# Attention, feed-forward and mixture of experts in one kernel: decay products moved from GpSimd to VectorE and ScalarE, routing of the last group moved and rearranged

## The chip, the cores and the metric

The kernel runs on one core of a Trainium2 chip. The metric is the time of one execution in microseconds of the device. Its engines are TensorE (matmuls, PE in the profile, its weight loads PEld), VectorE (DVE), ScalarE (ACT), GpSimd (POOL) and SyncE (SP), which issues most of the transfers. Each engine takes its instructions in order and waits where one needs what another has not finished.

## The reference

Three layers follow each other on B x S = 2 x 768 tokens of width 512 (8 heads of 64).

```python
# 1. linear attention with decay lam per head, in blocks
intra = (q k^T * Dmask) v                     # Dmask: lam ** (i - j), 0 above the diagonal
inter = (q * lam ** (i + 1)) state
state = lam ** block * state + (k * lam ** (block - 1 - j))^T v
# 2. feed-forward 512 -> 2048 -> 512
h = x @ w_in ; g = maximum(0.01 * h, h) ; x = g @ w_out        # weights are float64
# 3. eight experts, one per token
logits = x @ w_gate + modality_bias[modality_id]
e = argmax(logits) ; gate_w = softmax(logits)[e]
out = gate_w * (relu(x @ w1[e]) @ w2[e])
```

## The kernel before, in words

**Work and order.** The 1536 tokens are 12 chunks of 128, chunk 2j and 2j+1 make group j of 256 tokens. The feed-forward layer has 16 slices of 128 columns, so there are 96 units u = 16 j + f. The main loop goes over them; a unit is ff1 (12 matmuls, the fp32 product as three products of rounded parts, L406) into one of two banks, then L409 on ScalarE (0.01 h), L414 on VectorE (the maximum), L421 on ScalarE (the high part), L422 on VectorE (the low part), and, two units later, ff2 (6 matmuls, L435). Since the two banks alternate, ff1 of a unit waits for L414 of the unit two before it. The units of groups 0 and 1 alternate in the loop, the rest follow group by group. Nothing reorders the instructions: each engine's queue is as the code is written, and the engines run apart as far as the tiles allow.

**Conversion.** The feed-forward weights come as float64 bits and are turned into fp32 high and low parts inside the loop, one tile per unit from the fourth unit to the 26th (the "conversion ring" below): three bit steps on VectorE (L1494, L1499 twice), the rounding on ScalarE (L1504) and, one unit later, the difference on VectorE (L1506). The first tiles are converted ahead of the loop or several to a unit.

**Attention.** Its pieces are hooks: `at(j, f, fn, ...)` puts a call behind unit 16 j + f, called a slot here. `at_first` computes the scores of a chunk (L304), multiplies qT with the decay powers lq (`at_prep_q`, L281) and the scores with the decay matrix (`at_mask`, L317). `at_prep_k` multiplies k with its decay (L294 on GpSimd, L290 on ScalarE for chunks 2 and 3). `at_out` makes the chunk's output (L333, L343), which is staged (L345) or split into the parts xh and xl (L357, L358). `at_state` forms k^T v (L372) and multiplies the state with its decay (L378, GpSimd), `at_state_add` adds the two (L392). k and v have one buffer each, so that a chunk's k is loaded only after the state of the chunk before it has read its own. The two chunks of a group are dealt with in the group before.

**Routing.** Behind a group's last unit `evac_x2` copies its accumulators to the tile x2s (L461, L463) and writes them to memory. Since x2s has one buffer, the copy waits for what read the group before, its gate's write (L571) among it. The accumulators of odd groups lie in banks 3 and 4, those of even groups in 5 and 6, and the scores of later chunks take over such banks. `route_dot` makes the 16 dot products of a group with the gate's rows (two tiles, eight experts, L516), `route_v1` the one-hot of the largest, `route_rk` the ranks on TensorE from it (L546), `route_v2` the position from the ranks (L579 to L586), and `route_gate` the gate's factor (L561 to L571). RSLOT gives for each group the slot of its first dots, the step of experts per slot, the slot of v1, and the slot of the rest. In the last group of the main loop but one (group 4, whose dots fall into group 5's units), half of the dots are a product on GpSimd (L521) and a sum on ScalarE.

**First expert weights.** During group 5 the weights of the most frequent expert are loaded and split (`split_w`: L876 on ScalarE, L877 on VectorE or GpSimd), its tokens are indexed (`early_idx`), gathered (`first_gather`) and transposed (`TX`).

Of the kernel before, what the change touches and what calls it, by code (L numbers as in the profile page):

```python
# [21 lines left out]
C = 128  # L22
# [4 lines left out]
NSTAT = 10  # L27
NPLAIN = 12
NAR = 32
PREP_ACT = (2, 3)  # L30
KV = {1: 'wo15', 2: 'wi15', 3: 'wo14'}
QK = {2: 'wi14', 3: 'wo13'}
NPOS = {2: 0, 3: 1, 4: 2}
# [7 lines left out]
def tile_attention_ffn_moe(  # L41
# [235 lines left out]
    def at_prep_q(n):  # L277
        b, c = ORD[n]
        t = chunks[n]
        if c > 0:  # L280
            nc.gpsimd.tensor_mul(out=t["qT"], in0=t["qT"], in1=lq)  # L281

    def at_prep_k(n):
        b, c = ORD[n]
        t = chunks[n]
        if c + 1 >= NCH:
            return
        if n in PREP_ACT:
            for h in range(H):
                nc.scalar.activation(  # L290
                    out=t["k"][:, h, :], in_=t["k"][:, h, :], func=AF.Copy, scale=dec[:, h, C - 1:C]
                )
        else:
            nc.gpsimd.tensor_tensor(  # L294
                out=t["k"], in0=t["k"], in1=dec[:, :, C - 1:C].to_broadcast([128, H, D]), op=ALU.mult
            )

    def at_scores(n, b0, b1):
        t = chunks[n]
# [60 lines left out]
    def at_state(n, bk):  # L360
        b, c = ORD[n]
        if c + 1 >= NCH:
            return
        t = chunks[n]
        o = bank(bk, "as")
        kd = t["k"].rearrange("p h d -> p (h d)")
        vv = t["v"].rearrange("p h d -> p (h d)")
        for g in range(4):
            for half in range(2):
                p0 = half * 64  # L370
                cs = slice(g * 128 + p0, g * 128 + p0 + 64)
                nc.tensor.matmul(o[p0:p0 + 64, cs], lhsT=kd[:, cs], rhs=vv[:, cs], start=True, stop=True)  # L372
        t["so"] = o
        if c > 0:
            for half in range(2):
                p0 = half * 64
                sl = state[b][p0:p0 + 64, :, p0:p0 + 64]
                nc.gpsimd.tensor_tensor(  # L378
                    out=sl, in0=sl, in1=lq[p0:p0 + 64, :, C - 1:C].to_broadcast([64, 4, 64]), op=ALU.mult
                )  # L380

    def at_state_add(n):
# [126 lines left out]
    def route_dot(j, jobs):  # L509
        if j not in lgs:  # L510
            lgs[j] = sm.tile([128, 2, E], F32, tag="lgs", name="lgs")
        for e, tk, buf in jobs:
            xv = x2s[j][tk][:, 0:512]
            acc = lgs[j][:, tk, e:e + 1]
            if buf is None:
                nc.vector.scalar_tensor_tensor(  # L516
                    out=junk, in0=xv, scalar=1.0, in1=wgr[e], op0=ALU.mult, op1=ALU.mult, accum_out=acc
                )
            else:
                pr = qkv_p.tile([128, 512], F32, tag=buf, name="pr", bufs=1 if buf in ("v", "k") else 2)  # L520
                nc.gpsimd.tensor_mul(out=pr, in0=xv, in1=wgr[e])  # L521
                nc.scalar.activation(out=pr, in_=pr, func=AF.Copy, accum_out=acc)
# [769 lines left out]

    V, P = nc.vector, nc.gpsimd
    nc.sync.dma_start(out=lam_sb, in_=lam.rearrange("(h o) -> h o", o=1))
    load_chunk(0, ("qT", "kT"))
    load_win(0)
    make_dec()
    store_dec()
    load_wout(0)
# [76 lines left out]
        xt_split(n, chunks[n]["kT"])  # L1376

    at(0, 7, at_first, 4, 2, 7)
    at(0, 7, at_prep_k, 4)
    at(0, 8, at_out, 4, 7, True)  # L1380
    at(0, 9, at_state, 4, 2)
    at(0, 9, load_chunk, 5, ("v", "k"))
    at(0, 10, at_state_add, 4)
    at(0, 11, at_first, 5, 2, 7)
    at(0, 11, at_prep_k, 5)
    at(0, 12, at_out, 5, 7, True)
    at(0, 13, at_state, 5, 2)
    at(0, 14, at_state_add, 5)
# [3 lines left out]
    at(0, 15, load_chunk, 7, ("qT", "kT"))  # L1392


    at(2, 9, lambda: evac_x2(1))
    at(3, 2, lambda: evac_x2(2))

    SLOT = {
        2: (None, 2, 5, 7, 10, 10, 12, 13, 15),
# [1 line left out]
    for j in range(2, last):  # L1401
# [4 lines left out]
            at(j, s_ld, load_chunk, n, ("qT", "kT", "v", "k"))  # L1406
            at(j, s_ld, load_chunk, n + 1, ("qT", "kT"))
        at(j, s_a, at_first, n, *((2, 7) if j == 2 else sb))
        at(j, s_a, at_prep_k, n)
        at(j, s_o, at_out, n, 7)  # L1410
        at(j, s_s, at_state, n, 2)
        at(j, s_s, load_chunk, n + 1, ("v", "k"))
        at(j, s_s, at_prep_k, n + 1)
        at(j, s_d, at_state_add, n)
        at(j, s_a2, at_first, n + 1, *sb)
        at(j, s_o2, at_out, n + 1, 7)
# [1 line left out]
        at(j, s_d2, at_state_add, n + 1)  # L1418


    RSLOT = {0: (32, 1, 39, 40), 1: (41, 1, 48, 49), 2: (51, 1, 58, 59), 3: (66, 1, 73, 74), 4: (82, 2, 87, 88)}
    for r, (f0, step, fv, fr) in RSLOT.items():
        for i in range(0, E, step):
            jobs = [(e, tk, None) for e in range(i, i + step) for tk in range(2)]
            if r == last - 1:
                jobs = [(e, tk, ("v", "k")[e % 2] if tk else None) for e, tk, _ in jobs]
            at(0, f0 + i // step, route_dot, r, jobs)
        at(0, fv, route_v1, r)
        at(0, fr, route_rk, r, 7)
# [268 lines left out]
```

## Time and profile before

| | before |
|---|---|
| time, median of 3 runs | 526.44 us (526.16 to 526.71) |
| profiled execution | 525.76 us, of which the span is 523.7 |
| mean granted clock of TensorE | 0.979 |
| TensorE (PE) busy | 493.7 us, 94% |
| VectorE busy | 319.6 us, 61% |
| ScalarE busy | 174.1 us, 33% |
| GpSimd busy | 105.7 us, 20% |

The profile is of one execution, and its times count from the start of the span. Busy time is the time in which an engine worked; TensorE's can hold overlapped matmuls. The profile's rows give a number in brackets where an engine sat idle before an instruction, and what released it. A row of several instructions ("x4") has the time from the first one's start to the last one's end.

### The profile page before, as it was taken

The numbers are of one execution on the slowest core, as the hardware profiler recorded it, in microseconds if no ns is written. First come the engines' busy times: TensorE is split into PE (matmuls) and PEld (weight loads), VectorE is DVE, ScalarE is ACT, GpSimd is POOL, SyncE is SP. The second block draws the span as 40 slices with busy tenths as digits, with TensorE's granted clock in tenths as the row PEclk, the third lists the DMA queues.
The fourth block names the chain that finished last, engine by engine and source line by source line (L and its number), as shares of the span: only waits on it lengthen the run. The fifth ranks groups of instructions, "written<-read, shape, count | busy, mean of one in ns | idle before, by whom it ended". The sixth has DMA issues, their size and how long they took to land. (4 is left out here: it accounts for less than half of the span.)

```text
span 523.7 us, 9395 instructions
## 1 busy us (share of the span) xinstructions
PE 493.7 (94%) x3485; PEld 420.6 (80%) x3485; DVE 319.6 (61%) x767; ACT 174.1 (33%) x409; POOL 105.7 (20%) x142
## 2 busy tenths in 40 slices
PE   5769999999999999999999998999999999999994
PEld 3657978788988888888988897887788987879693
DVE  4798998998576787774577458864551252513130
ACT  2155434344322223223322335453222254322221
POOL 1220021212021211021022045260231212323111
PEclk8879999999999999999999998999999999999998
DMA  7999301703601102110400035211169509173101
GB/s 252 364 406 401 125 1 48 251 1 104 224 1 42 41 1 86 58 40 2 140 23 22 0 123 197 44 43 41 39 234 398 182 21 347 63 249 143 41 2 42
DMA packets 30667, 63.41 MB, mean 121 GB/s; under 512 B 6871, under 2 KB 8799, under 8 KB 30608
## 3 DMA queue, kind: packets, MB, share of 16 engines
q1 hardware_dynamic: 28496, 56.17, 30.5%
q0 software_dynamic: 2112, 6.52, 3.6%
q8 instruction: 29, 0.48, 0.4%
q14 instruction: 30, 0.25, 0.1%
HBM read 56.35 MB, written 6.52 MB: 120 GB/s over the span
## 5 line engine op out<-in xcount | busy, mean ns | idle before, releaser
L406 PE MATMUL hp<-xh,wi 128*128 128x256 f32 x768 | 127.4, 288 | 4.4 <-DVE t L414 2.7
L435 PE MATMUL x<-wo,gh 128*128 128x512 f32 x384 | 120.8, 396 | 1.0 <-DVE pm L317 1.0
L406 PEld LDWEIGHTS hp<-xh,wi 128*128 128x128 f32 x768 | 109.4, 192 | 13.2 <-DVE t L414 4.9
L435 PE MATMUL x<-wo,gl 128*128 128x512 f32 x192 | 75.8, 395 | 2.2 <-DVE gl L422 2.2
L435 PEld LDWEIGHTS x<-wo,gh 128*128 128x128 f32 x384 | 66.3, 190 | 9.3 <-PE hp L406 1.2
L421 ACT ACTIVATE gh<-t 128x256 fp32r<-128x256 f32 x96 | 40.1, 418 | 92.8 <-DVE t L414 92.8
L422 DVE TENSOR_TENSOR gl<-t,gh 128x256 fp32r<-128x256 f32 x96 | 46.3, 482 | 33.4 <-ACT gh L421 26.1
L406 PE MATMUL hp<-xl,wi 128*128 128x256 f32 x384 | 62.2, 285 | 0.0
L965 PE MATMUL hp<-xp,w1h 128*128 128x256 f32 x320 | 58.7, 284 | 0.0
L409 ACT ACTIVATE t<-hp 128x256 f32<-128x256 f32 x96 | 36.1, 376 | 62.8 <-PE hp L406 62.7
L414 DVE TENSOR_TENSOR t<-t,hp 128x256 f32<-128x256 f32 x96 | 40.0, 417 | 24.9 <-ACT t L409 23.5
L406 PEld LDWEIGHTS hp<-xl,wi 128*128 128x128 f32 x384 | 53.2, 192 | 0.4 <-DVE xl L358 0.4
L975 DVE SCALAR_TENSOR_TENSOR hp<-hp,hp 128x256 fp32r<-128x256 f32 x40 | 16.4, 423 | 60.1 <-ACT hp L974 29.3
L993 PE MATMUL o<-w2h,hp 128*128 128x512 f32 x160 | 52.5, 397 | 0.0
L965 PEld LDWEIGHTS hp<-xp,w1h 128*128 128x128 f32 x320 | 50.2, 192 | 2.6 <-issue 2.5
L435 PEld LDWEIGHTS x<-wo,gl 128*128 128x128 f32 x192 | 36.1, 188 | 14.2 <-DVE gl L422 6.3
L965 PE MATMUL hp<-xp,w1l 128*128 128x256 f32 x160 | 45.3, 283 | 0.0
L281 POOL TENSOR_TENSOR qT<-qT,lq 128x512 f32<-128x512 f32 x8 | 10.8, 1353 | 123.7 <-PE sc L304 97.7
L993 PEld LDWEIGHTS o<-w2h,hp 128*128 128x128 f32 x160 | 29.8, 188 | 7.0 <-issue 1.2
L993 PE MATMUL o<-w2l,hp 128*128 128x512 f32 x80 | 31.5, 393 | 0.0
L965 PEld LDWEIGHTS hp<-xp,w1l 128*128 128x128 f32 x160 | 30.7, 192 | 0.1
L516 DVE SCALAR_TENSOR_TENSOR junk<-x2s,wgr 128x512 bf16<-128x512 f32 x36 | 28.7, 796 | 0.6
(255 smaller groups left out, 657.6 us busy)
## 6 DMA issues: line engine op xcount, KB each, us to landing
rawi<-in_moe_w_in_dram SPq DMA_DIRECT2D x16, 512.0 KB, 8.2
rawo<-in_moe_w_out_dram SPq DMA_DIRECT2D x16, 512.0 KB, 7.1
raw<-in_moe_w_dram SPq DMA_DIRECT2D x16, 512.0 KB, 3.9
nr<-in_moe_w_dram SPq DMA_DIRECT2D x9, 512.0 KB, 12.2
xs_d<-x2s SPq DMA_DIRECT2D x12, 256.0 KB, 3.9
nrx<-in_moe_w_dram SPq DMA_DIRECT2D x6, 512.0 KB
wgr_hi<-in_moe_w_dram SPq DMA_DIRECT2D x6, 512.0 KB, 9.3
qT<-in_q_dram SPq DMA_DIRECT2D x10, 256.0 KB, 6.8
```

The costliest lines, as they stand in the source:

```text
L281: nc.gpsimd.tensor_mul(out=t["qT"], in0=t["qT"], in1=lq)
L406: nc.tensor.matmul(hp, lhsT=w[:, hl, kk, :], rhs=xx[:, kk, :], start=(n == 0), stop=(n == 11))
L409: nc.scalar.activation(out=t, in_=hp, func=AF.Copy, scale=0.01)
L414: nc.vector.tensor_max(out=t, in0=t, in1=hp)
L421: nc.scalar.activation(out=gh, in_=t, func=AF.Copy)
L422: nc.vector.tensor_sub(out=gl, in0=t, in1=gh.bitcast(F32))
L435: nc.tensor.matmul(x2[j][tk], lhsT=a[:, ts], rhs=wout[f][:, w, :], start=(f == 0 and n == 0), stop=(f == 15 and n == 2),)
L516: nc.vector.scalar_tensor_tensor(out=junk, in0=xv, scalar=1.0, in1=wgr[e], op0=ALU.mult, op1=ALU.mult, accum_out=acc)
L965: nc.tensor.matmul(hp.rearrange("p (a b) -> p a b", a=2), lhsT=w1s[kk][w][:, f * 128:(f + 1) * 128], rhs=x[:, :, ks], start=(n == 0), stop ...
L975: nc.vector.scalar_tensor_tensor(out=lo, in0=hp, scalar=0.0, in1=hi.bitcast(F32), op0=ALU.max, op1=ALU.subtract)
L993: nc.tensor.matmul(o2[b], lhsT=hT[b, f // 4][a][fs], rhs=w[:, f % 2, :], start=(n == 0), stop=(n == 23))
```

## The change

The change moves work between engines and slots:

- `at_prep_q` multiplies on VectorE instead of GpSimd, for ten chunks.
- `at_prep_k` multiplies on ScalarE for all chunks, head by head with a scale from memory. From chunk 4 on it comes in two halves of four heads, in two neighbouring slots.
- The state's decay in `at_state` is four ScalarE instructions over whole 128x128 tiles instead of two products on GpSimd.
- The dots of group 4 are all on VectorE, two in each of eight slots, instead of four in each of four slots, half of them on GpSimd.
- RSLOT: the ranks come two slots after v1 (one before) in groups 0 to 3; groups 1 and 2 begin one slot later. `evac_x2` of group 1 comes one slot later, of group 2 two.
- The first splits of expert weights are all on VectorE, in other slots; `early_idx` comes two slots later, gather and TX one.
- The first weight tile is loaded before chunk 0's q and k.

Line numbers of the changed kernel are 8 to 11 lower behind these functions: L399, L404, L411, L412 are the lines called L409, L414, L421, L422 above.

```diff
     def at_prep_q(n):
...
-            nc.gpsimd.tensor_mul(out=t["qT"], in0=t["qT"], in1=lq)
+            nc.vector.tensor_mul(out=t["qT"], in0=t["qT"], in1=lq)
...
-    def at_prep_k(n):
+    def at_prep_k(n, heads=range(H)):
...
-        if n in PREP_ACT:
-            for h in range(H):
-                nc.scalar.activation(
-                    out=t["k"][:, h, :], in_=t["k"][:, h, :], func=AF.Copy, scale=dec[:, h, C - 1:C]
-                )
-        else:
-            nc.gpsimd.tensor_tensor(
-                out=t["k"], in0=t["k"], in1=dec[:, :, C - 1:C].to_broadcast([128, H, D]), op=ALU.mult
-            )
+        for h in heads:
+            nc.scalar.activation(out=t["k"][:, h, :], in_=t["k"][:, h, :], func=AF.Copy, scale=dec[:, h, C - 1:C])
...
         if c > 0:
-            for half in range(2):
-                p0 = half * 64
-                sl = state[b][p0:p0 + 64, :, p0:p0 + 64]
-                nc.gpsimd.tensor_tensor(
-                    out=sl, in0=sl, in1=lq[p0:p0 + 64, :, C - 1:C].to_broadcast([64, 4, 64]), op=ALU.mult
+            for g in range(4):
+                nc.scalar.activation(
+                    out=state[b][:, g, :], in_=state[b][:, g, :], func=AF.Copy, scale=lq[:, g, C - 1:C]
                 )
...
+    load_win(0)
     load_chunk(0, ("qT", "kT"))
-    load_win(0)
...
     at(0, 7, at_first, 4, 2, 7)
-    at(0, 7, at_prep_k, 4)
+    at(0, 7, at_prep_k, 4, range(H // 2))
+    at(0, 8, at_prep_k, 4, range(H // 2, H))
     at(0, 8, at_out, 4, 7, True)
     at(0, 9, at_state, 4, 2)
...
     at(0, 11, at_first, 5, 2, 7)
-    at(0, 11, at_prep_k, 5)
+    at(0, 11, at_prep_k, 5, range(H // 2))
+    at(0, 12, at_prep_k, 5, range(H // 2, H))
...
-    at(2, 9, lambda: evac_x2(1))
-    at(3, 2, lambda: evac_x2(2))
+    at(2, 10, lambda: evac_x2(1))
+    at(3, 4, lambda: evac_x2(2))
 
     SLOT = {
         2: (None, 2, 5, 7, 10, 10, 12, 13, 15),
...
         at(j, s_s, load_chunk, n + 1, ("v", "k"))
-        at(j, s_s, at_prep_k, n + 1)
+        at(j, s_s, at_prep_k, n + 1, range(H // 2))
+        at(j, s_s + 1, at_prep_k, n + 1, range(H // 2, H))
         at(j, s_d, at_state_add, n)
         at(j, s_a2, at_first, n + 1, *sb)
...
-    RSLOT = {0: (32, 1, 39, 40), 1: (41, 1, 48, 49), 2: (51, 1, 58, 59), 3: (66, 1, 73, 74), 4: (82, 2, 87, 88)}
+    RSLOT = {0: (32, 1, 39, 41), 1: (42, 1, 49, 51), 2: (52, 1, 59, 61), 3: (66, 1, 73, 75), 4: (82, 1, 89, 90)}
     for r, (f0, step, fv, fr) in RSLOT.items():
         for i in range(0, E, step):
-            jobs = [(e, tk, None) for e in range(i, i + step) for tk in range(2)]
-            if r == last - 1:
-                jobs = [(e, tk, ("v", "k")[e % 2] if tk else None) for e, tk, _ in jobs]
+            jobs = [(e, tk) for e in range(i, i + step) for tk in range(2)]
             at(0, f0 + i // step, route_dot, r, jobs)
...
-        split_w(raw1[i], w1s[i], P if i in (1, 2) else V)
+        split_w(raw1[i], w1s[i], V)
...
-        split_w(raw2[i], w2s[i], P if i in (2,) else V)
+        split_w(raw2[i], w2s[i], V)
...
-    at(last, 9, early_idx)
-    at(last, 11, first_gather)
-    at(last, 14, TX, 0)
+    at(last, 11, early_idx)
+    at(last, 12, first_gather)
+    at(last, 15, TX, 0)
     for i in range(4):
-        at(last, (3, 13, 13, 13)[i], first_w1, i)
-        at(last, (7, 8, 9, 11)[i], first_w2, i)
+        at(last, (3, 13, 14, 15)[i], first_w1, i)
+        at(last, (6, 8, 10, 12)[i], first_w2, i)
```

ScalarE's queue in the conversion ring, around the scores of chunk 4; wi and wo are the rounded weight tiles. Before:

```order
L409 ACTIVATE t_821<-hp1_808 128x256
L421 ACTIVATE gh_829<-t_821 128x256
L1504 ACTIVATE wo8_833<-tw_823 128x512
L409 ACTIVATE t_854<-hp0_841 128x256
L421 ACTIVATE gh_862<-t_854 128x256
L1504 ACTIVATE wi9_866<-tw_856 128x512
L409 ACTIVATE t_907<-hp1_894 128x256
L421 ACTIVATE gh_915<-t_907 128x256
```

After:

```order
L399 ACTIVATE t_872<-hp0_859 128x256
L411 ACTIVATE gh_880<-t_872 128x256
L1495 ACTIVATE wi9_884<-tw_874 128x512
L288 ACTIVATE k_820<-k_820,dec_t_97 128x64 x4
L399 ACTIVATE t_928<-hp1_915 128x256
L411 ACTIVATE gh_936<-t_928 128x256
L1495 ACTIVATE wo9_940<-tw_930 128x512
L399 ACTIVATE t_961<-hp0_948 128x256
L411 ACTIVATE gh_969<-t_961 128x256
L1495 ACTIVATE wi10_973<-tw_963 128x512
L288 ACTIVATE k_820<-k_820,dec_t_97 128x64 x4
L337 COPY kT_816<-ao7_989 128x512
```

Between a rounding and the L409 (now L399) behind it the k products of chunk 4 have come, four at a time, and one unit later again; a few rows further down its queue the state's four decays stand in the same place.

ScalarE's queue in units 39 to 42, where ex is the exponential of group 0's gate and the last copy is that of group 1's accumulators. Before, from L409 of unit 39 on:

```order
L409 ACTIVATE t<-hp_1858 128x256
L421 ACTIVATE gh<-t 128x256
L409 ACTIVATE t<-hp_1912 128x256
L421 ACTIVATE gh<-t 128x256
L564 ACTIVATE ex,sums<-L,nmx 128x8 x2
L409 ACTIVATE t<-hp_1968 128x256
L421 ACTIVATE gh<-t 128x256
L461 COPY x2s<-x_611 128x512
```

After, from the decay of the state in slot 39 on:

```order
L368 ACTIVATE st_110<-st_110,lq 128x128 x4
L288 ACTIVATE k<-k,dec_t 128x64 x4
L399 ACTIVATE t<-hp_1960 128x256
L411 ACTIVATE gh<-t 128x256
L288 ACTIVATE k<-k,dec_t 128x64 x4
L399 ACTIVATE t<-hp_1990 128x256
L411 ACTIVATE gh<-t 128x256
L553 ACTIVATE ex,sums<-L,nmx 128x8 x2
L399 ACTIVATE t<-hp_2046 128x256
L411 ACTIVATE gh<-t 128x256
L451 COPY x2s<-x_629 128x512
```

The decay and the two halves of chunk 7's k product stand ahead of the next units' copies, and the exponential and the accumulators' copy are each one unit later.

VectorE's queue in the last group, around the first routing stage of group 4 (L531 to L538, now L520 to L527); w2l is a weight split. Before:

```order
L516 SCALAR_TENSOR_TENSOR junk,lgs<-x2s,wgr_hi 128x512 x2
L414 TENSOR_TENSOR t<-t,hp_3657 128x256
L422 TENSOR_TENSOR gl<-t,gh 128x256
L414 TENSOR_TENSOR t<-t,hp_3685 128x256
L422 TENSOR_TENSOR gl<-t,gh 128x256
L531 TENSOR_TENSOR L<-lgs,bsel 128x16
L532 TENSOR_REDUCE mx<-L 128x2
L534 SCALAR_TENSOR_TENSOR sc<-L,mx,rows_sb 128x8 x2
L537 TENSOR_REDUCE sx<-sc 128x2
L538 TENSOR_TENSOR oh<-sc,sx 128x16
L877 TENSOR_TENSOR w2l_3724<-raw_3655,w2h_3723 128x1024
```

After:

```order
L503 SCALAR_TENSOR_TENSOR junk,lgs<-x2s,wgr_hi 128x512 x2
L866 TENSOR_TENSOR w2l_3803<-raw_3733,w2h_3802 128x1024
L404 TENSOR_TENSOR t<-t,hp_3806 128x256
L412 TENSOR_TENSOR gl<-t,gh 128x256
L503 SCALAR_TENSOR_TENSOR junk,lgs<-x2s,wgr_hi 128x512 x2
L520 TENSOR_TENSOR L<-lgs,bsel 128x16
L521 TENSOR_REDUCE mx<-L 128x2
L523 SCALAR_TENSOR_TENSOR sc<-L,mx,rows_sb 128x8 x2
L526 TENSOR_REDUCE sx<-sc 128x2
L527 TENSOR_TENSOR oh<-sc,sx 128x16
L404 TENSOR_TENSOR t<-t,hp_3844 128x256
```

Before, one unit with no dots stood between the last dots and the routing stage; now the stage is directly behind the last dots, and a weight split stands one unit ahead of it.

## Rows read from the trace of the kernel before

**Rows 1.** The page, engines: busy us, share of the span, instructions.
```profile
PE 493.7 (94%) x3485; PEld 420.6 (80%) x3485; DVE 319.6 (61%) x767; ACT 174.1 (33%) x409; POOL 105.7 (20%) x142
```

**Rows 2.** Timeline, conversion ring: start, duration, engine, line, out<-in, [idle before <-releaser].
```profile
68.19 0.42 DVE L414 TENSOR_TENSOR t<-t,hp 128x256 f32<-128x256 f32 x1 [0.30 <-ACT t L409]
...
71.38 0.42 DVE L414 TENSOR_TENSOR t<-t,hp 128x256 f32<-128x256 f32 x1 [0.29 <-ACT t L409]
...
73.28 1.48 POOL L281 TENSOR_TENSOR qT<-qT,lq 128x512 f32<-128x512 f32 x1 [30.67 <-PE sc L304]
...
76.17 0.41 DVE L414 TENSOR_TENSOR t<-t,hp 128x256 f32<-128x256 f32 x1
...
83.36 0.42 DVE L414 TENSOR_TENSOR t<-t,hp 128x256 f32<-128x256 f32 x1 [0.30 <-ACT t L409]
...
86.56 0.57 ACT L345 COPY kT<-ao 128x512 f32<-128x512 f32 x1
...
87.44 0.42 DVE L414 TENSOR_TENSOR t<-t,hp 128x256 f32<-128x256 f32 x1 [0.78 <-ACT t L409]
...
94.31 0.54 PEld L406 LDWEIGHTS hp<-xh,wi 128*128 128x128 f32 x4 [0.30 <-DVE t L414]
```

**Rows 3.** Timeline, TensorE, two units in a row of group 4.
```profile
260.15 0.64 PE L406 MATMUL hp<-xh,wi 128*128 128x256 f32 x4
...
262.97 0.64 PE L406 MATMUL hp<-xh,wi 128*128 128x256 f32 x4
```

**Rows 4.** Start: the decay matrix's load (view of one tile), then the timeline.
```profile
L115 SPq DMA_DIRECT2D dec_t<-pw_d x2: 380/444/507, 7.2 to 7.6; - x2
...
DMA to landing us min/median/max: 4.9/4.9/4.9
...
13.33 2.48 DVE L317 TENSOR_TENSOR pm<-sc,dec_t 128x512 f32<-128x512 f32 x4
...
20.99 0.63 ACT L200 ACTIVATE wi<-tw 128x512 fp32r<-128x512 f32 x1 [2.55 <-DVE tw L191]
...
22.92 1.52 DVE L1494 TENSOR_SCALAR tw<-rawi 128x512 int32<-128x512 int32 x1
...
35.11 2.00 ACT L290 ACTIVATE kv<-kv,dec_t 128x64 f32<-128x64 f32 x8
```

**Rows 5.** Timeline, units 39 to 42.
```profile
165.67 1.15 SPq L154 DMA_DIRECT2D k<-in_k_dram  x1
...
166.93 0.39 ACT L409 ACTIVATE t<-hp 128x256 f32<-128x256 f32 x1 [1.91 <-PE hp L406]
...
169.30 0.17 DVE L579 TENSOR_TENSOR rm<-rk,oh 128x16 f32<-128x16 f32 x1
169.36 1.06 POOL L294 TENSOR_TENSOR k<-k,dec_t 128x512 f32<-128x512 f32 x1 [9.01 <-DMA k<-in_k_dram]
...
172.31 0.23 DVE L569 RECIPROCAL x2s<-sums 128x1 f32<-128x1 f32 x2 [1.14 <-POOL sums L567]
...
174.61 1.75 PE L304 MATMUL sc<-qT,kT 64*128 64x128 f32 x16 [0.40 <-ACT x2s L461]
```

**Rows 6.** Timeline, TensorE, the ranks of group 1.
```profile
200.23 0.18 PE L546 MATMUL rk<-oh,tri_b 128*128 128x8 bf16 x1 [1.02 <-DVE oh L538]
```

**Rows 7.** Timeline, a unit with two dots, and places of the last group.
```profile
161.56 0.42 DVE L414 TENSOR_TENSOR t<-t,hp 128x256 f32<-128x256 f32 x1
...
164.15 0.41 DVE L414 TENSOR_TENSOR t<-t,hp 128x256 f32<-128x256 f32 x1
...
321.24 1.22 PE L406 MATMUL hp<-xh,wi 128*128 128x256 f32 x4 [2.33 <-DVE t L414]
...
330.69 1.22 DVE L877 TENSOR_TENSOR w2l<-raw,w2h 128x1024 fp32r<-128x1024 f32 x1
...
340.50 0.40 PE L654 MATMUL pi<-eb,ohr 128*128 128x4 bf16 x10 [0.49 <-DVE eb L648]
```

**Rows 8.** Windows: length, busy (x) of PE, PEld, DVE, ACT, POOL, PEclk, DMA share, GB/s.
```profile
320.00:330.00 10.00, 8.76 (x49) 8.19 (x50) 7.93 (x20) 5.72 (x16) 3.23 (x2) 0.83 0.23 86
```

More of the change, by code (lines that the diff above doesn't have):

```diff
@@ L29 @@
 NAR = 32
-PREP_ACT = (2, 3)
 KV = {1: 'wo15', 2: 'wi15', 3: 'wo14'}
@@ L511, in route_dot @@
             lgs[j] = sm.tile([128, 2, E], F32, tag="lgs", name="lgs")
[L512 to L522, printed above, removed]
+        for e, tk in jobs:
+            nc.vector.scalar_tensor_tensor(
+                out=junk,
+                in0=x2s[j][tk][:, 0:512],
+                scalar=1.0,
+                in1=wgr[e],
+                op0=ALU.mult,
+                op1=ALU.mult,
+                accum_out=lgs[j][:, tk, e:e + 1],
+            )
     def route_v1(j):
@@ L1408, in tile_attention_ffn_moe @@
         at(j, s_a, at_first, n, *((2, 7) if j == 2 else sb))
-        at(j, s_a, at_prep_k, n)
+        at(j, s_a, at_prep_k, n, range(H // 2))
+        at(j, s_a + 1, at_prep_k, n, range(H // 2, H))
         at(j, s_o, at_out, n, 7)
```

## The prediction

> **What bounds the kernel now.** I read the engine table first: TensorE is busy 493.7 of 523.7 us [rows 1]. A change can give or cost time only where TensorE starts late, so the second view was TensorE's timeline, for its waits and their releasers. The change touches four kinds of place.
>
> First the conversion ring, 68 to 127 us. In each unit VectorE, ScalarE and VectorE again hand on: the last bit step on VectorE, the rounding (L1504) and L409 on ScalarE, L414 on VectorE. The pitch of L414 is 3.19 us there (68.19 to 71.38), each L414 waits 0.30 us for ScalarE, and the weight load of an ff1 waits for L414 in turn [rows 2]. An undisturbed unit of TensorE lasts 2.82 us (260.15 to 262.97) [rows 3]. So in this stretch TensorE follows the ring, and what lengthens either engine ahead of an L414 reaches the end of the kernel.
>
> Second the start, one chain through VectorE and ScalarE up to the fourth unit [rows 4]. Third the passage from group 1's accumulators to the scores of chunk 7 [rows 5]. Fourth TensorE's waits for routing: two of about 1.0 us, of which 200.23 is one [rows 6], and in the last group one of 2.33 and two of 0.5 to 0.6, of which 340.50 is one [rows 7], with a lower clock around the first [rows 8].
>
> **The ring.** Three things happen to it in each of chunks 4 and 5.
> (a) GpSimd's products leave. Around the one of 1.48 us at 73.28, L414 came 4.79 us after the one before it (71.38 to 76.17), 1.6 over the pitch. The state decay's share is read at 83.36 to 87.44: 4.08, which is 0.89 over, 0.48 of it the copy named under (c), so 0.4 [rows 2]. Together 2.0 per chunk go.
> (b) VectorE gets the q product, 128x512. A product of that kind and 128x1024 lasts 1.22 [rows 7], so half, 0.6, in a unit where L414 waits for nothing else.
> (c) ScalarE gets the k product in two halves, and the state decay. An instruction put ahead of L409 is paid in full: the copy of 0.57 at 86.56 raised L414's wait from 0.30 to 0.78 [rows 2]. Eight 64-wide k products took 2.00 [rows 4], so a half is 0.95 to 1.0. The first half stands in the unit that also has the q product and the masks; VectorE is the longer side there and hides it, and if that cover is missing it is 0.95 more. The second half costs 0.95. The state decay is four 128-wide instructions with a scale from memory, which no row shows: four 64-wide ones give 0.95 below, four of L409's 0.39 give 1.56 above [rows 4, 5]. I take 1.1, nearer to the instruction of the same form.
> Sum per chunk: -2.0 + 0.6 + 0.95 + 1.1 = +0.65, for two +1.3. Chunk 3's decay stands in the same way in the fourth unit: +1.1. If all that ScalarE gets were hidden, the two chunks would give 2.8.
>
> The Trainium skill (ScalarE: Activation LUTs, What ACT_TABLE_LOAD costs) prices an ACTIVATE at 186 ns plus 0.833 ns an element, 93 ns more for each pointer operand, 93 ns of overlap back to back. That makes an estimated 239 ns from one 64-wide product to the next, and the row's 2.00 for eight agrees. By the page four decays are an estimated 1.17 us, and the sum would be 0.3 higher.
>
> **The start.** With the first weight tile loaded first, the chain up to the masks at 13.33 moves forward by at most 0.8, since the decay matrix that the masks read lands at 7.6 + 4.9 = 12.5; I take 0.7. Chunk 0's q and k come later on SP's queue by one issue, and have that long. The k products of chunks 0 and 1 now stand on ScalarE ahead of the rounding at 20.99, which found 2.55 us of idle time before it. Sixteen of them are 3.8 us, so that rounding comes 3.8 - 2.55 - 0.7 = 0.5 later. Behind it two VectorE instructions lie beside GpSimd's q products; 22.92 is one, 1.52 instead of the 0.42 of L414's size, the other is like it: -2.2. The q products come to VectorE in their place: +1.2. At the masks of chunk 3 that is 0.5 - 2.2 + 1.2 = -0.5. Chunk 2's decay, 1.1 on ScalarE ahead of chunk 3's xh, makes it about +0.5 for the unit behind. The k products at 35.11 are on ScalarE in both kernels [rows 4]. With the ring: 0.5 + 1.1 + 1.3 = +2.9. Bounds: -3.5 (all of ScalarE's new work hidden, the start 0.7 earlier) and +5.7 (the two first halves paid as well, 1.9, and each decay at 1.4).
>
> **Units 39 to 42.** Before, chunk 7's k load is issued at 165.67, and GpSimd, which waits for it, starts its product at 169.36, while ScalarE runs L409 of unit 40 at 166.93. Group 0's second routing stage, which reads its ranks, starts at 169.30, the reciprocal of the gate comes at 172.31 after a wait of 1.14. The gate is written, the accumulators are copied out, and the scores that take over their banks start 2.30 after the reciprocal, at 174.61 [rows 5]. After, the first half of the k product stands on ScalarE behind its own load and ahead of L409 of unit 40. ScalarE is held to 169.36 + 0.95 = 170.3, and this L409 is 3.4 late. From there one chain: L409, L414 and L421 (to 171.5), the second half of k, L409 of unit 41 (to 172.6), its L414, L421 and L422 (to 173.95). VectorE comes to the second routing stage only then, and that takes 172.31 - 1.14 - 169.30 = 1.9, to 175.85. The scores start 2.30 later, at 178.15, which is 3.5 later than before. They keep their slot, so TensorE waits 3 us or more. The 1.75 for which they ran holds a wait for the second copy, some 0.5 that now falls into the longer wait: +3.0. The floor is the move of the ranks by one slot alone: 2.82 less the 1.14, +1.7. The ceiling is 2.82 and a half product, +3.8.
>
> Behind such a wait the clock falls. In the window from 320 to 330 us, which holds the wait of 2.33, the granted clock is 0.83, a mean of the levels 2.4 and 1.2 GHz: 0.17 x 10 = 1.7 us lost [rows 7, 8]. I add 1.7; the low end is 0. So this place is +4.7, from +1.7 to +5.5.
>
> The Trainium skill (DMA: Bandwidth & Descriptors, Anatomy of one DMA) gives a transfer 2.0 us plus its bytes over 436 GB/s, measured on another issue path: an estimated 2.6 us for this 256 KB tile. The row has 3.7 from issue to use, so it does not agree. By the page the hold would be 1.1 shorter and the total 1.1 lower.
>
> **Ranks of groups 1 and 2.** The one-hot that they wait for is made one slot before them now and two slots after the change. A slot is 2.82, the waits are 1.0: both go, -2.0 [rows 3, 6]. Nothing on TensorE is late next there.
>
> **The last group.** Before, half of its dots are on GpSimd, four to a slot; TensorE loses 2.33, 1.7 of clock, and 1.1 in the small waits: 5.1 [rows 7, 8]. After, VectorE has two dots in each of eight slots. A unit with two dots takes VectorE 2.59 (161.56 to 164.15) against 2.82, so 0.23 a unit is spare; three weight splits of 1.13 (330.69, less its overlap) fall into the same slots [rows 3, 7]. VectorE ends 3.4 - 8 x 0.23 = 1.6 behind. The first routing stage (1.1) comes behind the last two dots, in the slot before the ranks, which leaves it short by the 1.6 and some 0.8 that two dots and the stage take beyond a slot: a wait of 2.4 at the ranks, and a lower clock again, 1.2 of it inside this group. That is 3.6, net -1.5, between -5.1 (the dots keep up) and 0.
>
> **Sum** against the profiled execution (525.76, of which 2.06 lie around its span; the median is 0.68 above it): 2.9 + 4.7 - 2.0 - 1.5 = +4.1, so 529.9 there and 530.5 as a median.
>
> **Rivals.** (1) Faster: ScalarE is busy 33% [rows 1], and what it gets finds room. Then the start and ring give 3.5, the ranks 2.0, the last group 1.5 to 5.1, and units 39 to 42 cost 1.7: -5.3 to -8.9, 517.5 to 521; with half of that room about -2, 524.5. It is decided by L414's waits for ScalarE, which would stay at 0.30; the row with 0.78 speaks against it. (2) The k load does not lengthen the chain, and no clock is lost: 1.7 instead of 4.7, total +1.1, 527.5. For it: the scores' wait before was only 0.40 [rows 5]. (3) The last group's dots keep up: -5.1 instead of -1.5, total +0.5, 527, no change. (4) Slower still: the first halves of k are paid in the ring (+1.9) and the last group gives nothing (+1.5): 534.
>
> **How the numbers follow.** A difference under 0.2% (1.05 us) can't be told from none here. Chances: the forecast 0.43, with its own range of 528.5 to 532.5; rival 1 0.18; rival 2 0.16; rival 3 0.12; rival 4 0.11. Slower gets the forecast, rival 4 and rival 2 (at its bound): 0.70. Same gets rival 3 but for 0.01: 0.11. Faster gets rival 1 and that: 0.19. The range from 524.5 to 533.5 leaves out the far part of rivals 1 and 4.
>
> **What would show it.** In the ring, L414's waits for ScalarE rise to about 1.4 in the units with decays, and the pitch of the unit with the q product falls below 4.8. In units 39 to 42 TensorE waits some 3 us at the scores for the copy of the accumulators, with a lower clock behind it. The ranks of groups 1 and 2 wait for nothing. The last group has no wait of 2.33 for L414 and one of about 2.4 at the ranks. I am wrong if L414 keeps waiting 0.30 us in the ring, or if L409 of unit 40 runs before the k load lands.

## The result and the profile after

The changed kernel takes 533.3 us (median of 4 runs, 532.42 to 534.13) against 526.47 us for the one before: a ratio of 1.013, with a 95% interval of 1.0112 to 1.0147. It is slower, as forecast; 530.5 was the prediction. The profiled execution took 532.42, its span is 530.5 us, 6.8 longer than before.

The page's engine row answers to [rows 1]:

```profile
PE 499.1 (94%) x3485; PEld 425.7 (80%) x3485; DVE 316.2 (60%) x796; ACT 194.8 (37%) x489; POOL 49.7 (9%) x97
```

GpSimd's 105.7 us have become 49.7, ScalarE's 174.1 have become 194.8, VectorE's work has hardly changed. TensorE is as full as before, and its span is longer. To see where, both traces are cut at the first weight load of ff1 of a few units; each column is the time between two such cuts, in us, with the experiments of the next section in the other rows.

| kernel | start to unit 12 | 12-28 (ring) | 28-40 | 40-44 | 44-49 | 49-61 | 61-80 | 80 to end |
|---|---|---|---|---|---|---|---|---|
| before | 68.66 | 58.43 | 38.03 | 13.87 | 17.02 | 43.49 | 62.11 | 222.10 |
| after | 71.27 | 59.89 | 38.02 | 19.45 | 17.02 | 42.30 | 62.33 | 220.22 |
| difference | +2.61 | +1.46 | 0 | +5.58 | 0 | -1.19 | +0.22 | -1.88 |
| k later | 71.84 | 59.86 | 38.03 | 14.65 | 17.02 | 42.37 | 62.33 | 220.20 |
| old slots | 70.19 | 59.88 | 38.02 | 14.32 | 17.02 | 46.47 | 62.12 | 220.39 |
| decay on GpSimd | 68.79 | 58.38 | 38.03 | 18.60 | 17.02 | 42.62 | 62.33 | 220.13 |
| last group alone | 69.14 | 58.44 | 38.03 | 15.19 | 17.02 | 43.48 | 62.11 | 220.09 |
| q on VectorE alone | 68.92 | 57.49 | 38.03 | 14.36 | 17.02 | 44.39 | 62.11 | 221.98 |
| ranks alone | 71.31 | 58.52 | 38.03 | 14.18 | 17.02 | 40.94 | 62.33 | 222.16 |
| mended | 67.50 | 58.45 | 38.03 | 12.84 | 17.02 | 40.94 | 62.33 | 219.78 |

The table also says what may be read from it. Up to unit 39 the rows "before", "last group alone" and "ranks alone" are the same code, and they reach unit 12 between 68.66 and 71.31; three with the changed kernel's code reach it between 70.19 and 71.84. A single trace settles nothing under 2.5 us in the first column, and about 1.3 in the column 40-44 (13.87 to 15.19 in the same three kernels). The other columns repeat within 0.1 us where the code is the same.

Both spreads can be placed. The first goes with TensorE's granted clock from 40 to 50 us: in nine of the fourteen traces of this document it is 1.00 there, and these reach unit 12 by 69.14; "after", "k later", "old slots" and "ranks alone" have 0.83 or 0.84 and reach it at 70.19 or later; the mended version with later splits has 0.97 and reaches it at 69.46. What is lost ahead of 40 us varies too and does not order the traces so. The second is the wait at chunk 7's scores, 0.40 us in "before" and 1.71 in "last group alone", with the same code up to there.

**The ring.** The timeline of the changed kernel at the place of [rows 2]; the engine and line stand behind the duration, what the engine waited for at the end:

```profile
77.19 0.42 DVE L404 TENSOR_TENSOR t<-t,hp 128x256 f32<-128x256 f32 x1 [0.30 <-ACT t L399]
...
81.81 0.41 DVE L404 TENSOR_TENSOR t<-t,hp 128x256 f32<-128x256 f32 x1
...
85.00 0.42 DVE L404 TENSOR_TENSOR t<-t,hp 128x256 f32<-128x256 f32 x1 [0.30 <-ACT t L399]
...
89.63 0.42 DVE L404 TENSOR_TENSOR t<-t,hp 128x256 f32<-128x256 f32 x1 [1.73 <-ACT t L399]
...
95.62 1.26 ACT L368 ACTIVATE st<-st,lq 128x128 f32<-128x128 f32 x4
...
96.79 0.36 ACT L399 ACTIVATE t<-hp 128x256 f32<-128x256 f32 x1
...
97.19 0.42 DVE L404 TENSOR_TENSOR t<-t,hp 128x256 f32<-128x256 f32 x1 [1.46 <-ACT t L399]
```

The unit with the q product and the masks and the one behind it last 77.19 to 85.00, 7.81 us. Before, the unit beside GpSimd's products and the masks' unit behind it lasted 71.38 to 80.17, 8.79:

```profile
74.72 1.24 POOL L294 TENSOR_TENSOR k<-k,dec_t 128x512 f32<-128x512 f32 x1
...
80.17 0.41 DVE L414 TENSOR_TENSOR t<-t,hp 128x256 f32<-128x256 f32 x1
```

VectorE gained the 1.0 that (a) and (b) give, but not from the q product alone: GpSimd's k product stands right behind it in [rows 2], in the same unit, and has left GpSimd as well. And L404 waits for ScalarE 1.73 us where the second half of k stands together with the staged copy, and 1.46 where the decay stands, against 0.78 and 0.30. The four decays take 1.26, and L399 starts 1.17 after their start; the prediction had 1.1. The estimate from the Trainium skill (ScalarE: Activation LUTs, What ACT_TABLE_LOAD costs), 1.17, agrees with this row.

**The start**, answering to [rows 4]:

```profile
12.84 2.48 DVE L309 TENSOR_TENSOR pm<-sc,dec_t 128x512 f32<-128x512 f32 x4 [1.56 <-DMA dec_t<-pw_d]
...
18.21 2.01 ACT L288 ACTIVATE k<-k,dec_t 128x64 f32<-128x64 f32 x8
...
20.12 2.02 ACT L288 ACTIVATE kv<-kv,dec_t 128x64 f32<-128x64 f32 x8
...
22.03 0.63 ACT L199 ACTIVATE wi<-tw 128x512 fp32r<-128x512 f32 x1
...
41.46 1.26 ACT L368 ACTIVATE st<-st,lq 128x128 f32<-128x128 f32 x4
...
43.26 0.74 PE L396 MATMUL hp<-xh,wi 128*128 128x256 f32 x4 [2.04 <-ACT xh L349]
```

The masks come only 0.5 earlier (12.84 for 13.33), and they do wait for the decay matrix. The k products on ScalarE end where the rounding starts, at 22.03 for 20.99. Chunk 2's decay at 41.46 stands ahead of the xh for which the fourth unit's ff1 waits 2.04 us; that wait was 0.96 before. Behind it the clock is lower. The windows from 40 to 50 us, before and after (length, busy time of the engines, granted clock third from the end):

```profile
40.00:50.00 10.00, 9.04 (x72) 7.80 (x71) 8.25 (x18) 5.75 (x16) 1.23 (x2) 1.00 1.03 398
...
40.00:50.00 10.00, 7.96 (x57) 6.42 (x54) 6.60 (x14) 6.70 (x20) 0.00 (x0) 0.83 1.04 399
```

A mean of 0.83 of its two levels, 2.4 and 1.2 GHz, is 0.17 x 10 = 1.7 us lost.

**Units 39 to 43**, answering to [rows 5]:

```profile
169.73 0.37 SPq L153 DMA_DIRECT2D k<-in_k_dram  x1
...
173.42 1.07 ACT L288 ACTIVATE k<-k,dec_t 128x64 f32<-128x64 f32 x4 [3.17 <-DMA k<-in_k_dram]
...
174.39 0.36 ACT L399 ACTIVATE t<-hp 128x256 f32<-128x256 f32 x1
...
178.17 0.17 DVE L568 TENSOR_TENSOR rm<-rk,oh 128x16 f32<-128x16 f32 x1
...
179.39 0.21 DVE L558 RECIPROCAL x2s<-sums 128x1 f32<-128x1 f32 x2
...
181.68 2.67 PE L296 MATMUL sc<-qT,kT 64*128 64x128 f32 x16 [3.34 <-ACT x2s L451]
```

ScalarE stands still for 3.17 us until the k load lands, and L399 of unit 40 follows at 174.39. The second routing stage starts at 178.17, the reciprocal follows at 179.39, the scores start 2.29 later and wait 3.34 us. Behind that the clock is lower. The windows, the last being the one of [rows 8]:

```profile
180.00:190.00 10.00, 8.32 (x44) 7.63 (x45) 6.91 (x16) 1.76 (x4) 0.20 (x2) 0.66 0.15 53
...
181.20:188.00 6.80, 6.32 (x31) 5.81 (x32) 5.00 (x11) 0.81 (x2) 0.10 (x2) 0.50 0.20 77
...
320.00:330.00 10.00, 10.00 (x64) 9.03 (x63) 8.27 (x24) 3.83 (x8) 0.21 (x1) 1.00 0.84 308
```

From 180 to 190 us the granted clock is 0.66, which is 0.34 x 10 = 3.4 us lost in that window. All of it lies ahead of unit 44, which starts at 188.6: from 181.2 to 188.0 the clock is 0.50, the lower level. From 320 to 330 us, where the wait of 2.33 is gone, the clock is 1.00 instead of 0.83.

**A wait that was not forecast**, at the scores of chunk 8:

```profile
218.14 0.59 ACT L451 COPY x2s<-x 128x512 f32<-128x512 f32 x1 [0.59 <-DMA xs_d<-x2s]
...
218.75 1.00 SPq L455 DMA_DIRECT2D xs_d<-x2s  x2
...
220.31 0.45 SPq L153 DMA_DIRECT2D kT<-in_kt_dram  x1
...
224.46 1.16 PE L296 MATMUL sc<-qT,kT 64*128 64x128 f32 x16 [1.27 <-DMA kT<-in_kt_dram]
```

Group 2's accumulators are copied at 218.14, and their write to memory stands on SP's queue ahead of chunk 8's loads. So kT is issued 4.1 us ahead of the scores, which wait 1.27 of it; in the kernel before it was issued 8 us ahead of them:

```profile
206.70 0.44 SPq L154 DMA_DIRECT2D kT<-in_kt_dram  x1
...
214.65 1.16 PE L304 MATMUL sc<-qT,kT 64*128 64x128 f32 x16
```

**The last group**, where the ranks wait instead of ff1 [rows 7]:

```profile
343.97 0.17 PE L535 MATMUL rk<-oh,tri_b 128*128 128x8 bf16 x1 [2.28 <-DVE oh L527]
```

Behind that wait the clock is lower again, as forecast; the window, which has 1.00 before:

```profile
340.00:350.00 10.00, 7.72 (x45) 6.69 (x44) 7.82 (x29) 3.42 (x10) 1.30 (x4) 0.83 0.02 1
```

### The profile page after: what moved, and what is told of

It reads as the page before. It is cut to its first block, busy times and chain, and to the rows that moved or that the text cites. A ratio compares the mean times of both kernels' runs of the same rounds, so it can differ in the third digit from the quotient of the medians.

```text
span 530.5 us, 9446 instructions
## 1 busy us (share of the span) xinstructions
PE 499.1 (94%) x3485; PEld 425.7 (80%) x3485; DVE 316.2 (60%) x796; ACT 194.8 (37%) x489; POOL 49.7 (9%) x97
## 5 line engine op out<-in xcount | busy, mean ns | idle before, releaser
L425 PE MATMUL x<-wo,gh 128*128 128x512 f32 x384 | 122.8, 402 | 1.7 <-DVE pm L309 1.7
L396 PEld LDWEIGHTS hp<-xh,wi 128*128 128x128 f32 x768 | 110.6, 194 | 14.2 <-DVE t L404 4.7
L425 PEld LDWEIGHTS x<-wo,gh 128*128 128x128 f32 x384 | 67.4, 194 | 10.2 <-issue 1.9
L411 ACT ACTIVATE gh<-t 128x256 fp32r<-128x256 f32 x96 | 40.1, 418 | 81.9 <-DVE t L404 81.9
L404 DVE TENSOR_TENSOR t<-t,hp 128x256 f32<-128x256 f32 x96 | 40.2, 419 | 34.2 <-ACT t L399 32.9
L412 DVE TENSOR_TENSOR gl<-t,gh 128x256 fp32r<-128x256 f32 x96 | 40.7, 424 | 33.4 <-ACT gh L411 26.1
L399 ACT ACTIVATE t<-hp 128x256 f32<-128x256 f32 x96 | 36.2, 377 | 63.6 <-PE hp L396 63.2
L963 ACT ACTIVATE hp<-hp 128x256 fp32r<-128x256 f32 x40 | 15.2, 384 | 41.2 <-PE hp L954 40.9
L503 DVE SCALAR_TENSOR_TENSOR junk<-x2s,wgr_hi 128x512 bf16<-128x512 f32 x40 | 27.5, 689 | 0.7
```

The source lines that it names most:

```text
L396: nc.tensor.matmul(hp, lhsT=w[:, hl, kk, :], rhs=xx[:, kk, :], start=(n == 0), stop=(n == 11))
L399: nc.scalar.activation(out=t, in_=hp, func=AF.Copy, scale=0.01)
L404: nc.vector.tensor_max(out=t, in0=t, in1=hp)
L411: nc.scalar.activation(out=gh, in_=t, func=AF.Copy)
L412: nc.vector.tensor_sub(out=gl, in0=t, in1=gh.bitcast(F32))
L425: nc.tensor.matmul(x2[j][tk], lhsT=a[:, ts], rhs=wout[f][:, w, :], start=(f == 0 and n == 0), stop=(f == 15 and n == 2),)
```

## The experiments

Each edit is to the changed kernel ("after") or to the kernel before. Ratios are to the kernel before in the same runs. Of the line RSLOT a few cuts show only the groups whose numbers change.

**k later** (after):

```diff
-        at(j, s_s, at_prep_k, n + 1, range(H // 2))
-        at(j, s_s + 1, at_prep_k, n + 1, range(H // 2, H))
+        at(j, s_s + 2, at_prep_k, n + 1, range(H // 2))
+        at(j, s_s + 3, at_prep_k, n + 1, range(H // 2, H))
```

> The changed kernel (533.3) with the k products of the second chunk of a group two slots later, where its load has long landed. Theory (the k load holds ScalarE in unit 40 and with it the chain to the accumulators' copy): L399 of unit 40 runs right behind its matmuls again, the wait of 3.34 at chunk 7's scores falls under 1.2, the low clock behind it goes, the time falls by 3 to 5.5 us, to 528 to 530.5. Rival (the ranks and the copy, one slot later, set the wait by themselves): the wait stays above 2.5 and the time within 1 us of 533.3.

528.61 us (ratio 1.003, 1.0008 to 1.0053): 4.7 less than the changed kernel. L399 of unit 40, the scores, and the window behind them:

```profile
171.54 0.39 ACT L399 ACTIVATE t<-hp 128x256 f32<-128x256 f32 x1 [0.73 <-PE hp L396]
...
180.00 1.76 PE L296 MATMUL sc<-qT,kT 64*128 64x128 f32 x16 [1.30 <-ACT x2s L451]
```

```profile
180.00:190.00 10.00, 9.88 (x80) 8.61 (x81) 7.40 (x18) 2.76 (x9) 0.00 (x0) 1.00 0.14 54
```

L399 waits for nothing but its matmuls, the scores wait 1.30 instead of 3.34 (the expectation said under 1.2), and the clock stays at 1.00. The column 40-44 falls from 19.45 to 14.65 and no other but the first moves by more than 0.1. The k load's hold is shown.

**Old slots** (after):

```diff
-    at(2, 10, lambda: evac_x2(1))
-    at(3, 4, lambda: evac_x2(2))
+    at(2, 9, lambda: evac_x2(1))
+    at(3, 2, lambda: evac_x2(2))
...
-    RSLOT = {0: (32, 1, 39, 41), 1: (42, 1, 49, 51), 2: (52, 1, 59, 61), 3: (66, 1, 73, 75), 4: (82, 1, 89, 90)}
+    RSLOT = {0: (32, 1, 39, 40), 1: (41, 1, 48, 49), 2: (51, 1, 58, 59), 3: (66, 1, 73, 74), 4: (82, 1, 89, 90)}
```

> The changed kernel with the slots of the routing of groups 0 to 3 and of the accumulators' copies as before; the k products stay as changed. Theory (both the k load and the later slot lengthen the chain): the wait at chunk 7's scores is about 1.4, the wait of 1.27 at chunk 8's scores goes, the ranks of groups 1 and 2 wait again by about 1.0 each; in all 2 to 3.5 us less, 530 to 531.5. Rival (the k load alone): the wait stays above 2.5, the time falls by at most 0.5 or rises.

530.51 us (1.0084, 1.0056 to 1.0113). The k product, the scores, the two ranks, and the window behind the scores:

```profile
171.62 1.07 ACT L288 ACTIVATE k<-k,dec_t 128x64 f32<-128x64 f32 x4 [2.47 <-DMA k<-in_k_dram]
...
178.02 1.76 PE L296 MATMUL sc<-qT,kT 64*128 64x128 f32 x16 [0.79 <-ACT x2s L451]
...
203.79 0.18 PE L535 MATMUL rk<-oh,tri_b 128*128 128x8 bf16 x1 [1.16 <-DVE oh L527]
...
239.33 0.18 PE L535 MATMUL rk<-oh,tri_b 128*128 128x8 bf16 x1 [2.30 <-DVE oh L527]
...
180.00:190.00 10.00, 10.00 (x77) 8.87 (x77) 8.38 (x21) 2.78 (x7) 0.00 (x0) 1.00 0.03 9
```

ScalarE is held here too (2.47 us idle before k, 3.17 in the changed kernel), yet the scores wait only 0.79. So neither cause makes the long wait alone: the column 40-44 is 0.4 over before with the hold alone and 0.8 with the later slots alone, both within its spread, and 5.6 with both. The columns read as if each had slack ahead of it that the other uses up, and here the low clock came with the long wait alone. What the old slots cost is the column 49-61: 46.47, since the ranks wait 1.16 and 2.30 again, with a granted clock of 0.83 from 240 to 250 us behind the second (1.7 us). The wait at chunk 8's scores is gone, as expected.

**Decay on GpSimd** (after):

```diff
-            for g in range(4):
-                nc.scalar.activation(
-                    out=state[b][:, g, :], in_=state[b][:, g, :], func=AF.Copy, scale=lq[:, g, C - 1:C]
+            for half in range(2):
+                p0 = half * 64
+                sl = state[b][p0:p0 + 64, :, p0:p0 + 64]
+                nc.gpsimd.tensor_tensor(
+                    out=sl, in0=sl, in1=lq[p0:p0 + 64, :, C - 1:C].to_broadcast([64, 4, 64]), op=ALU.mult
```

> The changed kernel with the state's decay on GpSimd again. Theory (what ScalarE gets ahead of L399 is paid in full, GpSimd beside VectorE costs 0.4): -1.2 each for chunks 2 and 3, -0.76 each for chunks 4 and 5, in all 3.9 less, 529.4; the wait of L404 for ScalarE is 0.3 to 0.4 in these units. Rival (GpSimd costs VectorE as much as ScalarE's place in the ring does): within 1 us of 533.3.

528.87 us (1.0054, 1.0034 to 1.0074), 4.4 less than after. L404, here L406, in the unit that had waited 1.46 us and the one ahead of it:

```profile
90.74 0.42 DVE L406 TENSOR_TENSOR t<-t,hp 128x256 f32<-128x256 f32 x1 [0.30 <-ACT t L401]
...
93.93 0.42 DVE L406 TENSOR_TENSOR t<-t,hp 128x256 f32<-128x256 f32 x1 [0.30 <-ACT t L401]
```

The wait is 0.30 and the pitch 3.19 instead of 4.36. The ring's column falls by 1.5, two chunks of 0.76 as expected, and the first column by 2.5 in this trace, where the clock from 40 to 50 us is 1.00 again. At chunk 7's scores this trace has the same wait as the changed kernel, with half the clock lost behind it:

```profile
177.93 2.19 PE L296 MATMUL sc<-qT,kT 64*128 64x128 f32 x16 [3.34 <-ACT x2s L453]
...
175.00:185.00 10.00, 6.97 (x43) 6.30 (x44) 7.28 (x20) 1.80 (x4) 0.20 (x2) 0.83 0.15 53
```

That is 1.7 us instead of 3.4, and the column 40-44 is 18.60 instead of 19.45.

**Last group alone** (before, with the changed route_dot, group 4's slots, splits, indexing, gather and transpose):

```diff
-4: (82, 2, 87, 88)
+4: (82, 1, 89, 90)
...
-        at(last, (3, 13, 13, 13)[i], first_w1, i)
-        at(last, (7, 8, 9, 11)[i], first_w2, i)
+        at(last, (3, 13, 14, 15)[i], first_w1, i)
+        at(last, (6, 8, 10, 12)[i], first_w2, i)
```

> The kernel before with the change of the last group alone (dots of group 4, weight splits, indexing, gather, transpose). Theory: the wait of 2.33 goes, one of about 2.8 at the ranks comes; 1.4 less, 525.0. Rival (the parts of the change are worth nothing on their own here): within 0.5 of 526.4.

524.65 us (0.9961, 0.9946 to 0.9977). The part is a gain of 1.9 (1.4 was expected), and the last column says the same, 222.10 to 220.09.

**q on VectorE alone** (before):

```diff
-            nc.gpsimd.tensor_mul(out=t["qT"], in0=t["qT"], in1=lq)
+            nc.vector.tensor_mul(out=t["qT"], in0=t["qT"], in1=lq)
```

> The kernel before with the q products on VectorE and nothing else changed; the k products and the decay stay on GpSimd. Theory (a product on VectorE costs 0.6, beside GpSimd's it cost 1.1): two at the start -0.9, two in the ring -0.5 each, 1.5 to 2 less, 524.7. Rival (GpSimd's k product only moves, and takes as much from VectorE as both did): within 0.5 of 526.4.

525.48 us (0.9986, 0.9968 to 1.0004): not told from none, where 1.5 to 2 was expected. The ring gave its share (58.43 to 57.49), but in the column 49-61 nearly all of it goes again, since the one-hots come later and their ranks wait 1.34 and 1.56:

```profile
200.37 0.18 PE L546 MATMUL rk<-oh,tri_b 128*128 128x8 bf16 x1 [1.34 <-DVE oh L538]
...
235.17 0.18 PE L546 MATMUL rk<-oh,tri_b 128*128 128x8 bf16 x1 [1.56 <-DVE oh L538]
```

**Ranks alone** (before):

```diff
-    at(3, 2, lambda: evac_x2(2))
+    at(3, 3, lambda: evac_x2(2))
...
-1: (41, 1, 48, 49), 2: (51, 1, 58, 59), 3: (66, 1, 73, 74)
+1: (41, 1, 48, 50), 2: (52, 1, 59, 61), 3: (66, 1, 73, 75)
```

> The kernel before with the ranks of groups 1 to 3 two slots after their one-hot, and group 2's copy one slot later (51); group 0 and its copy as before. Theory (a unit ahead of these ranks lost 1.5, the wait of 1.0 with what is behind it; chunk 8's loads wait only if the copy comes at 52): 3.0 less, no new wait at chunk 8's scores, 523.4. Rival (the later copy holds chunk 8's load here too): the scores of chunk 8 wait over 1 us, 524.5 or more.

524.23 us (0.9957, 0.9937 to 0.9977), 2.2 less (3.0 was expected). Its write, chunk 8's kT and the scores:

```profile
209.52 0.97 SPq L465 DMA_DIRECT2D xs_d<-x2s  x2
...
211.03 0.45 SPq L154 DMA_DIRECT2D kT<-in_kt_dram  x1
...
216.53 1.16 PE L304 MATMUL sc<-qT,kT 64*128 64x128 f32 x16
```

With the copy at 51 the load is issued 5.5 us ahead of the scores, and these wait for nothing. The columns 49-61 and 61-80 give 2.55 - 0.22 = 2.3; after has 1.19 - 0.22 = 1.0, and 1.3 between them is the wait of chunk 8.

**First weight tile first** (before, that edit alone):

> The kernel before with the first weight tile loaded ahead of chunk 0's q and k, nothing else. Theory (the masks wait for the decay matrix then, so the front moves by 0.5 at most): 0 to 0.7 less, not told from none. Rival (the later q and k delay the scores): 0.5 more or worse.

525.23 us (0.998, 0.9966 to 0.9994): a little better than expected, 0.3 to 1.8 less. Its trace reaches unit 12 at 68.95, so where it came from stays open.

**Three parts together** (before, with q on VectorE, ranks alone, last group alone), then the same with the second weights' splits later, then with group 4's ranks and the gather one slot later:

```diff
-        at(last, (6, 8, 10, 12)[i], first_w2, i)
+        at(last, (10, 11, 12, 13)[i], first_w2, i)
...
-4: (82, 1, 89, 90)
+4: (82, 1, 89, 91)
...
-    at(last, 12, first_gather)
+    at(last, 13, first_gather)
```

> The kernel before with three parts together: q products on VectorE, ranks of groups 1 to 3 as in the run with these alone, and the change of the last group. If the parts add up: -1.7 - 3.0 - 1.9 = -6.6, 519.8. Rival (their gains overlap): above 521.5.

520.67 us (0.9882, 0.9847 to 0.9918): 5.8 less. Alone the parts gave 0.9, 2.2 and 1.9, which is 5.0; what the q products cost at the ranks is gone once these stand a slot later (column 49-61: 40.94).

> The same three parts, with the splits of the second weights in slots 10 to 13 instead of 6, 8, 10 and 12. Theory (the wait of 2.3 at group 4's ranks is the dots and three splits in one stretch): that wait falls under 0.6, 1 to 2 us less than the other, 518 to 519. Rival (the splits are then late for the end): the time is the same or longer.

519.72 us (0.9876, 0.9839 to 0.9913). The ranks, and a place behind the last unit:

```profile
328.80 0.17 PE L545 MATMUL rk<-oh,tri_b 128*128 128x8 bf16 x1 [0.27 <-DVE oh L537]
...
348.25 0.50 PE L929 MATMUL h<-w1h,xgh 128*128 128x512 f32 x1 [1.56 <-ACT xgh L915]
```

The wait at the ranks fell from 2.73 to 0.27, but the first expert matmul now waits 1.56 for a ScalarE copy; its queue and VectorE's have the later splits ahead of that copy. The column 80 to end is 220.28, for 220.54 without the edit: most of the gain was given back, and in these two traces the shorter time is the start's (67.26 for 68.88).

> The best version so far (519.7) with group 4's ranks one slot later (91) and the gather's permutation one slot later (slot 13). Theory (its waits of 0.27 at the ranks and 0.88 at the permutation go): 1 us less, 518.7. Rival (the gather's transfer is then late for the transpose in slot 15): 520 or more.

520.6 us (0.9893, 0.9876 to 0.991), where the rival had put it. The waits of 0.27 and 0.88 are gone, and the transpose waits for the gather instead:

```profile
346.81 0.66 PE L912 MATMUL gt<-id_sb,xgp 128*128 128x128 f32 x4 [1.99 <-DMA xgp<-xs_d,gidx]
```

But the column 80 to end is 220.15, for 220.28 without the edit: next to nothing, and the longer time of this trace is the start's (68.78 for 67.26).

**Mended** (after, with the edit of "k later" and the decay on GpSimd, group 0's old slots, the ranks of group 1 at 50 and group 2's copy at 51):

> The changed kernel with its three costs taken out: second chunk's k products two slots later, the state's decay on GpSimd, group 0's ranks and copy in their old slots, group 1's ranks at 50 and group 2's copy at 51. Theory (the loss is these three and what is left of the change gains): 4.7 + 4.4 less and chunk 8's wait of 1.3 gone, 521 to 523, under the kernel before. Rival (something else of the change also costs): above 525.

519.13 us (0.9868, 0.985 to 0.9886): faster than both kernels by 7.3 and 14.2, and more than expected. The scores of chunk 7 wait for nothing, and one wait is left at the ranks of group 4:

```profile
173.05 1.16 PE L296 MATMUL sc<-qT,kT 64*128 64x128 f32 x16
...
330.79 0.17 PE L537 MATMUL rk<-oh,tri_b 128*128 128x8 bf16 x1 [2.27 <-DVE oh L529]
```

> The mended version of the changed kernel (519.1) with the splits of the second expert weights in slots 10 to 13. Theory (as in the kernel before: three splits between the dots make the wait of 2.27 at group 4's ranks): that wait falls under 0.6, 1 us less, 518.1. Rival (the end of the group takes it back, since other waits there grow by as much): 519 or more.

520.86 us (0.9882, 0.9843 to 0.9922), not better; its four runs spread from 519.44 to 522.52, and the trace is of the slowest. The ranks' wait went, and the first expert matmul waits as it did in the kernel before with the same edit:

```profile
330.75 0.17 PE L537 MATMUL rk<-oh,tri_b 128*128 128x8 bf16 x1 [0.26 <-DVE oh L529]
...
350.18 0.50 PE L921 MATMUL h<-w1h,xgh 128*128 128x512 f32 x1 [1.52 <-ACT xgh L907]
```

The column 80 to end is 221.42, 1.6 more than without the edit. Behind the wait of 1.52 the granted clock is 0.83 from 350 to 360 us, 1.7 us lost, where the mended version has 1.00.

## Why the prediction was right, step by step

The direction, the places and most prices held; the sum was 4.1 and came out at 6.8. The result lies inside the stated range by 0.2, but outside the 528.5 to 532.5 that the forecast gave itself: the range held it because it reached nearly to rival 4, and that rival's two grounds did not come about. By the columns the sum is short by 1.2 at the start and the ring, by 0.9 in units 39 to 42 and by 1.0 at the ranks; the last group gave 0.4 more than forecast.

- **The ring**, +1.3: it was +1.46. The decay's term is shown by a single edit, 1.5 for two chunks. That of the q product was right only together with k's: alone it gave 0.95 for two chunks, half of the 2.0 that (a) and (b) make of it. The other half came with the k product, whose move cost 58.38 - 57.49 = 0.9 ("decay on GpSimd" less "q on VectorE alone"), not two second halves of 0.95.
- **The start with chunk 3's decay**, 0.5 + 1.1: the traces differ by 2.6, no more than the same code does. The step that failed is the forward move of 0.7: the masks came 0.5 earlier and the second xh on ScalarE, behind which the k products stand, 0.1 (17.71 for 17.84), so that the rounding came 1.0 later instead of 0.5. And the sum has no term for the clock here. The decays' share, 2.5 in one trace, is larger than the two of 1.1, and up to 1.7 of it can be the clock between 40 and 50 us. All three traces with the decays on ScalarE have that loss, but "ranks alone" has it without them, so whether the decays bring it stays open.
- **Units 39 to 42**, +4.7: it was +5.6. The wait grew by 3.34 - 0.40 = 2.9, as worked out, though from a chain that was 0.5 too long: from the second routing stage to the reciprocal it took 1.2 us, not 1.9. The term for the clock was too small: 1.7 was taken and 3.4 were lost, of which the column shows 5.58 - 2.94 = 2.6. With the decay on GpSimd the same wait lost the 1.7, so one earlier window could not fix that term. The experiments add what the prediction did not say: the floor of 1.7 for the slots alone was too high, 0.8 was measured. Before, the gate's first step on GpSimd came at 170.82, right behind the k product there, and that wait is gone too; this reason is read from the trace and was not tried.
- **The ranks**, -2.0: -2.3 with the ranks alone. The prediction's sentence that nothing on TensorE is late next was wrong: the copy moved with the ranks, chunk 8's loads stand behind its write on SP's queue, and 1.3 came back. That queue was to be walked through, and for group 2 I did not.
- **The last group**, -1.5: -1.9, with a wait of 2.28 where 2.4 was forecast. The 1.2 taken for the clock behind it is not seen: the changed kernel has 0.83 from 340 to 350 us and "last group alone" 1.00, with last columns 0.1 apart.
- **Rivals.** L404's waits of 1.46 and 1.73 rule out the first, the k experiment the second, the ranks of group 4 the third. The fourth's place, the first halves of k, cost nothing: L404 at 81.81, behind the q product and the masks, does not wait for ScalarE. And the last group gave its 1.9.
- **The rule on transfers** (the Trainium skill, DMA: Bandwidth & Descriptors, Anatomy of one DMA): the k load again took 3.7 us, 169.73 to 173.42, not the 2.6 estimated from it.

## What to carry to other kernels

Work moved to an engine that is idle on average is paid in full where that engine is a link between two others; read the wait of the next link there, not the busy share. Where another link is the longer one, as VectorE was beside the first halves of k, it is free. An instruction that waits for a load holds all that is queued behind it, so put it where its load has long landed. Two delays that each fit into slack can together make a wait that is longer than both, and lower the clock as well; undo them one at a time before judging either.

## What the runs showed of the hardware

At chunk 7's scores the granted clock stayed at 1.00 behind waits of 0.40 to 1.71 us, in seven traces. Behind a wait of 3.34 us it fell, with 3.4 us lost in one trace and 1.7 in another. Behind a wait of 2.27 or 2.28 us at the ranks of group 4 it fell in four traces ("after", "k later", "old slots", "decay on GpSimd") and stayed at 1.00 in two ("last group alone", "mended"). So a single trace does not price the clock behind a wait of such a length. And the same code reached unit 12 at times up to 2.65 us apart, the latest with a clock of 0.84 from 40 to 50 us, where the others have 1.00.
